# Loading wqk over two DMA queues, the second held by a memset, in a gated linear-attention and SwiGLU kernel

## The chip, the cores and the metric

The kernel runs on one core of a Trainium2 chip. The metric is the device time of one launch in microseconds; a lower one is better. The profile is a trace of one execution, with times in microseconds from the start of its span.

The engines are named as in the profile: PE is TensorE's matmuls and PEld its weight loads, DVE is VectorE, ACT is ScalarE, POOL is GpSimd, SP is SyncE. A "q" behind the name (SPq, ACTq) is that engine's sequencer, which issues DMAs in program order.

## The reference

One input `x` of 2048 tokens by 512 features feeds two branches, which a gate mixes. All tensors are bf16.

```python
def _A_ref(x, wqkv, wo):                      # linear attention, 32 heads of 16
    qkv = (x @ wqkv).reshape(B, S, 3, H, Dh).transpose(2, 0, 3, 1, 4)
    phi = lambda t: where(t > 0, t + 1, exp(t)) + 1e-6
    pq, pk = phi(q), phi(k)
    kv, z = einsum("bhsd,bhse->bhde", pk, v), einsum("bhsd->bhd", pk)
    o = einsum("bhqd,bhde->bhqe", pq, kv) / (einsum("bhqd,bhd->bhq", pq, z)[..., None] + 1e-6)
    return o.transpose(0, 2, 1, 3).reshape(B, S, D) @ wo

def _B_ref(x, w1, w3, w2):                    # SwiGLU, F = 1376
    return (silu(x @ w1) * (x @ w3)) @ w2

g = sigmoid((x * gate_w).sum(-1, keepdims=True))
return g * _A_ref(x, wqkv, wo) + (1 - g) * _B_ref(x, w1, w3, w2)
```

## The kernel before

The program is traced with a schedule written by hand: each engine runs its instructions in the order of the source, and semaphores are added where one engine reads or overwrites what another (or a DMA) has written. The contraction dimension of 512 is cut into KC = 4 pieces of 128, called kc below, and the tokens into NT = 16 tiles of 128.

**The start, up to about 9 us.** This is the stretch that the change touches. POOL makes small constants (`ident`, `ones`, the block mask `bmask` by a memset and two affine selects at L74 to L79, and the zeroed `hrem` tiles). SP issues the first DMAs in this order: the first 256 tokens of `x` in their natural layout (`xN`, L116), then the weights for q and k in four pieces of 128 rows by 1024 columns (`load_wqk`, L113, 256 KB each), then for each token tile from 2 to 15 a transposing DMA (`load_xT`, L110) with the natural rows of `x` in between (L128), then `wr`, `w1`, `w3`, `wv`, `wo` and `w2`. On ACT's own queue stands one small DMA, `touch` (L120), which reads 32 bytes from each row of wqkv's second and third piece; nothing reads the tile that it fills.

ACT loads its table and runs one tiny exponential (`act_pre`, L117) ahead of that DMA in program order. PE starts with 13 matmuls on constants (`warm_step`, L315). When `xN` is there, PE transposes the first two token tiles by matmuls with the identity (L321); DVE and ACT copy them from PSUM to `xT` (L335 to L338, and L350 for the last piece). Then come the projections of tiles 0 and 1 (L167), ordered by the weight piece that they need: for kc 0 the four of k and q, the transposes of kc 3, for kc 1 the four of k and q, then k alone for kc 2 (two matmuls), and k alone for kc 3. So each piece of `wqk` has a first reader: the 1st, the 5th, the 9th and the 11th projection matmul.

**After the start.** The projections, phi and the accumulation of the attention's G matrix (`g_step`) run token tile by token tile up to about 46 us. Then four token blocks of 512 run the SwiGLU (`glu_step`, which reads `w1` at L262 and `w3` at L268) and the outputs (`out_step`), with the attention's small products in between.

**DMA bookkeeping.** A DMA raises one of eight semaphores (102 to 109 in the trace), used in turn. From the ninth DMA on, an issue first waits for the landing of the DMA eight places before it.

Of the kernel before, what the change touches and what calls it, by code (L numbers as in the profile page):

```python
# [12 lines left out]
BF16 = mybir.dt.bfloat16  # L13
# [3 lines left out]
def kernel(  # L17
# [17 lines left out]
    nc = tc.nc  # L35
    P = nc.NUM_PARTITIONS

    Bb, S, D = A_x.shape
# [3 lines left out]
    KC = D // P  # L42
# [14 lines left out]
    wqkv_r = A_wqkv.rearrange("(kc d) n -> d kc n", d=P)  # L57
    w1_r = B_w1.rearrange("(kc d) f -> d kc f", d=P)
    w3_r = B_w3.rearrange("(kc d) f -> d kc f", d=P)

    consts = ctx.enter_context(tc.tile_pool(name="consts", bufs=1))
# [8 lines left out]

    ones = consts.tile([P, P], BF16, name="ones")
    nc.gpsimd.memset(ones[:], 1.0)
    bmask = consts.tile([P, HPC, Dh], BF16, name="bmask")
    nc.gpsimd.memset(bmask[:], 1.0)  # L74
    nc.gpsimd.affine_select(
        out=bmask[:], in_=bmask[:], pattern=[[-Dh, HPC], [0, Dh]], compare_op=ALU.is_ge,
        fill=0.0, base=0, channel_multiplier=1,
    )
    nc.gpsimd.affine_select(  # L79
        out=bmask[:], in_=bmask[:], pattern=[[Dh, HPC], [0, Dh]], compare_op=ALU.is_ge,  # L80
        fill=0.0, base=Dh - 1, channel_multiplier=-1,
# [10 lines left out]


    xN = consts.tile([P, NT, D], BF16, name="xN")
    wqk = consts.tile([P, KC, 2 * D], BF16, name="wqk")
    wq = wqk[:, :, 0:D]
    wk = wqk[:, :, D : 2 * D]
    wv = consts.tile([P, KC, D], BF16, name="wv")
# [2 lines left out]
    w1 = consts.tile([P, KC, F0], BF16, name="w1")  # L101
    w3 = consts.tile([P, KC, F0], BF16, name="w3")
# [3 lines left out]
    dq = nc.sync  # L106
# [3 lines left out]
        dq.dma_start(out=xT[:, :, ts], in_=x2d[ts, :], transpose=True)  # L110

    def load_wqk(kc):
        dq.dma_start(out=wqk[:, kc, :], in_=wqkv_r[:, kc, 0 : 2 * D])  # L113

    x_first = x2d[0 : 2 * P, :].rearrange("(p j) d -> p j d", j=2)
    dq.dma_start(out=xN[:, 0:2, :], in_=x_first)  # L116
    nc.scalar.activation(out=act_pre[:], in_=warm[:, 0:1], func=ACT.Exp)  # L117

    touch = consts.tile([P, 2, 16], BF16, name="touch")
    nc.scalar.dma_start(out=touch[:], in_=wqkv_r[:, 1:3, 0:16])  # L120
    for kc in range(KC):
        load_wqk(kc)
    natural = {3: (2, 4), 5: (4, 8), 7: (8, 12), 11: (12, 16)}
# [5 lines left out]
    with nc.allow_non_contiguous_dma(reason="gate column"):  # L129
        dq.dma_start(  # L130
            out=wr[:, :, 2 * FR : NR], in_=gate_w.rearrange("(kc d o) -> d kc o", d=P, o=1)
        )
    dq.dma_start(out=wr[:, :, 0:FR], in_=w1_r[:, :, F0:F])
    dq.dma_start(out=wr[:, :, FR : 2 * FR], in_=w3_r[:, :, F0:F])
    for w, w_r, cuts in ((w1, w1_r, (0, KC)), (w3, w3_r, (0, 2, KC))):
        for a, b in zip(cuts, cuts[1:]):
            dq.dma_start(out=w[:, a:b, :], in_=w_r[:, a:b, 0:F0])
    dq.dma_start(out=wv[:], in_=wqkv_r[:, :, 2 * D : 3 * D])
    dq.dma_start(out=wo[:], in_=A_wo.rearrange("(kc d) n -> d kc n", d=P))
# [358 lines left out]
```

## Time and profile before

| | |
|---|---|
| time, median of 3 runs | 179.68 us (179.66 to 179.94) |
| the profiled execution's own time | 179.22 us |
| its span, first to last instruction | 177.5 us |
| PE busy | 173.9 us (98%) |
| DVE, ACT, POOL busy | 100.5, 62.3, 62.9 us |
| mean DMA rate | 85 GB/s |
| granted TensorE clock | 1.0 in all slices |

The profiled execution's time is 1.72 us more than its span (launch and end) and 0.46 us less than the median. The page gives the busy share of each engine, the share of the DMA engines and the chain of work that ended last; a timeline gives the instructions of a stretch in order, each with the idle time of its engine before it and what ended that idle time in brackets. An issue's "us to landing" runs from its start on the issuing engine until its semaphore is complete.

### The profile page before, as it was taken

What the parts mean: (1) busy time and instruction counts of PE and PEld (TensorE: products, weight loads), DVE (VectorE), ACT (ScalarE), POOL (GpSimd) and SP (SyncE); (2) the same over time, 40 slices, a digit from 0 to 9 for tenths busy, and PEclk for the clock granted to TensorE, in tenths of its full rate; (3) what the DMA queues carried; (4) which work ended last, traced back from release to release, by engine and by line L of the source; (5) the groups of instructions that cost most, each with busy time, mean ns of one, the idle gap of its engine ahead of it and who ended that gap; (6) DMA issues with size and microseconds to landing.
All of it is one profiled execution on the core that took longest, in us unless ns stands there. A gap on an engine that the chain in (4) does not pass through costs nothing.

```text
span 177.5 us, 2504 instructions
## 1 busy us (share of the span) xinstructions
PE 173.9 (98%) x880; PEld 84.1 (47%) x880; DVE 100.5 (57%) x195; ACT 62.3 (35%) x113; POOL 62.9 (35%) x105
## 2 busy tenths in 40 slices
PE   8999999999999999999999999999999999999993
PEld 5444444444454464644444464444445444444453
DVE  1399788888899663575434166634325664433222
ACT  3354544444735441332342223142322223342130
POOL 5086656656577240446200044540004432000000
PEclk9999999999999999999999999999999999999999
DMA  5989869994002120233100013520000342000001
GB/s 174 269 202 216 163 106 264 406 381 142 4 0 59 30 47 16 59 82 96 30 0 4 0 40 80 90 63 0 0 0 30 89 92 59 0 0 0 30 33 59
DMA packets 28940, 15.15 MB, mean 85 GB/s; under 512 B 20896, under 2 KB 27264, under 8 KB 28928
## 3 DMA queue, kind: packets, MB, share of 16 engines
q1 hardware_dynamic: 28656, 14.98, 32.3%
q8 instruction: 7, 0.11, 0.3%
q14 instruction: 5, 0.04, 0.1%
q10 hardware_dynamic: 272, 0.01, 0.1%
HBM read 8.43 MB, written 2.10 MB: 59 GB/s over the span
## 4 chain that ended last, share of the span: by engine, by line
PE 98%; DVE 0%; issue 0%
PE bank L427 21%; PE bank L262 19%; PE bank L268 19%; PE bank L167 16%; PE bank L414 8%; PE bank L215 8%; PE bank L229 3%; PE bank L315 2%; PE bank L389 1%; PE bank L402 0%; PE bank L321 0%; DVE o L431 0%; PE bank L376 0%
## 5 line engine op out<-in xcount | busy, mean ns | idle before, releaser
L274 DVE TENSOR_TENSOR hT<-bank,sg 128x512 bf16<-128x512 f32 x40 | 27.2, 681 | 30.9 <-PE bank L268 30.9
L268 PE MATMUL bank<-xT,w 128*128 128x512 bf16 x160 | 41.1, 379 | 0.0
L262 PE MATMUL bank<-xT,w 128*128 128x512 bf16 x160 | 41.1, 379 | 0.0
L427 PE MATMUL bank<-w,hT 128*128 128x512 bf16 (+3 forms) x198 | 40.7, 355 | 0.0
L273 ACT ACTIVATE sg<-bank 128x512 bf16<-128x512 f32 x40 | 23.9, 597 | 46.9 <-PE bank L262 46.9
L296 POOL TENSOR_TENSOR pqs<-pq,rden 128x512 bf16<-128x512 bf16 x16 | 16.9, 1055 | 65.1 <-issue 60.0
L167 PE MATMUL bank<-wqk,xT 128*128 128x512 bf16 x128 | 30.6, 382 | 0.0
L431 DVE SCALAR_TENSOR_TENSOR o<-bank,omg_all,aga 128x512 bf16<-128x512 f32 (+2 forms) x18 | 12.5, 692 | 28.1 <-PE bank L427 28.0
L427 PEld LDWEIGHTS <-hT 128*128 128x128 bf16 (+1 forms) x198 | 18.5, 98 | 19.8
L199 POOL TENSOR_TENSOR zacc<-zacc,pk 128x128 f32<-128x128 f32 x56 | 23.3, 446 | 10.4 <-DVE pk L185 10.4
L268 PEld LDWEIGHTS <-w 128*128 128x128 bf16 x160 | 15.7, 98 | 18.9
L262 PEld LDWEIGHTS <-w 128*128 128x128 bf16 x160 | 15.6, 98 | 18.5
L419 ACT ACTIVATE aga<-bank,g_all 128x512 f32<-128x512 f32 x16 | 11.0, 687 | 28.9 <-PE bank L414 28.9
L167 PEld LDWEIGHTS <-xT 128*128 128x128 bf16 x128 | 12.5, 98 | 15.0 <-issue 0.5
L281 POOL TENSOR_TENSOR pr<-pq,zb 128x512 f32<-128x512 bf16 x16 | 18.4, 1153 | 1.7 <-DVE zb L377 1.7
L414 PE MATMUL bank<-M,pqT 128*128 128x512 bf16 x64 | 16.4, 378 | 0.0
L215 PE MATMUL bank<-pk,xN 128*128 128x512 bf16 x64 | 16.4, 379 | 0.0
L180 ACT ACTIVATE eq<-bank 128x512 bf16<-128x512 f32 x16 | 9.4, 597 | 16.0 <-PE bank L167 16.0
L185 DVE SCALAR_TENSOR_TENSOR pk<-bank,emk 128x512 bf16<-128x512 f32 x16 | 11.1, 692 | 1.6
L180 ACT ACTIVATE ek<-bank 128x512 bf16<-128x512 f32 x16 | 9.4, 597 | 6.6 <-PE bank L167 6.6
L185 DVE SCALAR_TENSOR_TENSOR pq<-bank,emq 128x512 bf16<-128x512 f32 x16 | 11.1, 692 | 0.6
L285 DVE TENSOR_REDUCE den<-pr 128x32 f32<-128x512 f32 x16 | 10.8, 676 | 0.0
(50 smaller groups left out, 81.7 us busy)
## 6 DMA issues: line engine op xcount, KB each, us to landing
w<-in_B_w_dram SPq DMA_DIRECT2D x4, 640.0 KB, 9.6
out_dram<-o SPq DMA_DIRECT2D x15, 128.0 KB, 1.9
xN<-in_A_x_dram SPq DMA_DIRECT2D x3, 512.0 KB, 4.5
w<-in_B_w_dram SPq DMA_DIRECT2D x1, 1280.0 KB, 7.6
wqk<-in_A_wqkv_dram SPq DMA_DIRECT2D x4, 256.0 KB, 3.7
xN<-in_A_x_dram SPq DMA_DIRECT2D x2, 256.0 KB, 2.9
wv<-in_A_wqkv_dram SPq DMA_DIRECT2D x1, 512.0 KB, 10.7
wo<-in_A_wo_dram SPq DMA_DIRECT2D x1, 512.0 KB, 11.1
```

The lines of the kernel that those rows point to most:

```text
L167: nc.tensor.matmul(ps[:], lhsT=xT[:, kc, t * P : (t + 1) * P], rhs=w[:, kc, :], start=(kc == 0), stop=(kc == KC - 1),)
L180: nc.scalar.activation(out=e[:], in_=ps[:], func=ACT.Exp)
L185: nc.vector.scalar_tensor_tensor(out=dst, in0=ps[:], scalar=0.0, in1=em[:], op0=ALU.max, op1=ALU.add)
L199: nc.gpsimd.tensor_tensor(out=(zaccb if t == NT - 1 else zacc)[:, cs], in0=zacc[:, cs], in1=pk[t][:, cs], op=ALU.add,)
L215: nc.tensor.matmul(bank[kc][:], lhsT=xN[:, t, kc * P : (kc + 1) * P], rhs=pk[t][:], start=(t == 0), stop=(t == NT - 1),)
L262: nc.tensor.matmul(g_ps[:], lhsT=w1[:, kc, fs], rhs=xT[:, kc, tok], start=(kc == 0), stop=(kc == KC - 1),)
L268: nc.tensor.matmul(u_ps[:], lhsT=w3[:, kc, fs], rhs=xT[:, kc, tok], start=(kc == 0), stop=(kc == KC - 1),)
L273: nc.scalar.activation(out=sg[:], in_=g_ps[:], func=ACT.Silu)
L274: nc.vector.tensor_tensor(out=hT[tb][:, fc, :], in0=u_ps[:], in1=sg[:], op=ALU.mult)
L281: nc.gpsimd.tensor_tensor(out=pr[t][:], in0=pq[:, t, :], in1=zb[:], op=ALU.mult)
L414: nc.tensor.matmul(a_ps[:], lhsT=pqT[:, c, ts], rhs=M2[:, c, :], start=(c == 0), stop=(c == KC - 1),)
L427: nc.tensor.matmul(b_ps[:, 0:w], lhsT=hT[tb][:n, fc, tl], rhs=w2[:n, fc, cs], start=(fc == 0), stop=(fc == FC),)
```

## The change

`wqk`'s pieces 1 and 3 are issued from ACT's queue, pieces 0 and 2 stay on SP's. A memset of one column of piece 1 is put on POOL, behind `bmask`'s first affine select. It writes where piece 1's DMA writes, so this DMA waits for it, and piece 3, which is next on ACT's queue, stands behind that wait. The DMA `touch` is left out. `w1` is loaded in two DMAs, kc 0 and 1 and then kc 2 and 3, as `w3` already is, in place of one; the number of DMAs stays the same.

```diff
     ones = consts.tile([P, P], BF16, name="ones")
     nc.gpsimd.memset(ones[:], 1.0)
+    wqk = consts.tile([P, KC, 2 * D], BF16, name="wqk")
     bmask = consts.tile([P, HPC, Dh], BF16, name="bmask")
     nc.gpsimd.memset(bmask[:], 1.0)
     nc.gpsimd.affine_select(
         out=bmask[:], in_=bmask[:], pattern=[[-Dh, HPC], [0, Dh]], compare_op=ALU.is_ge,
         fill=0.0, base=0, channel_multiplier=1,
     )
+
+    nc.gpsimd.memset(wqk[:, 1, 0:1], 0.0)
     nc.gpsimd.affine_select(
...
-    wqk = consts.tile([P, KC, 2 * D], BF16, name="wqk")
...
     def load_wqk(kc):
-        dq.dma_start(out=wqk[:, kc, :], in_=wqkv_r[:, kc, 0 : 2 * D])
+        q = nc.scalar if kc % 2 else dq
+        q.dma_start(out=wqk[:, kc, :], in_=wqkv_r[:, kc, 0 : 2 * D])
 
     x_first = x2d[0 : 2 * P, :].rearrange("(p j) d -> p j d", j=2)
     dq.dma_start(out=xN[:, 0:2, :], in_=x_first)
     nc.scalar.activation(out=act_pre[:], in_=warm[:, 0:1], func=ACT.Exp)
-
-    touch = consts.tile([P, 2, 16], BF16, name="touch")
-    nc.scalar.dma_start(out=touch[:], in_=wqkv_r[:, 1:3, 0:16])
     for kc in range(KC):
         load_wqk(kc)
...
-    for w, w_r, cuts in ((w1, w1_r, (0, KC)), (w3, w3_r, (0, 2, KC))):
-        for a, b in zip(cuts, cuts[1:]):
+    for w, w_r in ((w1, w1_r), (w3, w3_r)):
+        for a, b in ((0, 2), (2, KC)):
             dq.dma_start(out=w[:, a:b, :], in_=w_r[:, a:b, 0:F0])
```

## The prediction

> **What bounds the kernel now.** I read the page first, for the engine that sets the time.
>
> ```profile
> span 177.5 us, 2504 instructions
> PE 173.9 (98%) x880; PEld 84.1 (47%) x880; DVE 100.5 (57%) x195; ACT 62.3 (35%) x113; POOL 62.9 (35%) x105
> q10 hardware_dynamic: 272, 0.01, 0.1%
> ```
>
> PE is busy 98% of the span, and it also makes up 98% of the chain that ended last. A change of DMA queues leaves PE's work as it is, so it can only take or add PE's idle time. q10 is ACT's queue; it carries `touch` alone. Next I read the chain in order of time, for its first microseconds.
>
> ```profile
> 0.83 2.93 PE bank L315 x13
> 3.76 0.64 PE bank L321 x6
> 4.41 1.30 PE bank L167 x4
> 5.71 0.11 PE bank L321 x2
> 5.82 1.29 PE bank L167 x6
> ```
>
> The chain is PE's alone: 13 warm-up matmuls, 6 transposes, 4 projections of kc 0, 2 transposes, the projections of kc 1 and on. From 5.82 on there is one projection every 0.215 us (1.29 / 6). What PE waited for inside this is in the timeline of the same stretch.
>
> ```profile
> 0.80 0.40 SPq L116 DMA_DIRECT2D xN<-in_A_x_dram  x1
> 0.85 0.43 ACTq L120 DMA_DIRECT2D touch<-in_A_wqkv_dram  x1
> 1.25 1.83 SPq L113 DMA_DIRECT2D wqk<-in_A_wqkv_dram  x4
> 1.72 0.34 POOL L75 TENSOR_SCALAR_AFFINE_SELECT bmask<-bmask 128x128 bf16<-128x128 bf16 x1
> 3.13 2.58 SPq L110 DMA_TRANSPOSE xT<-in_A_x_dram  x2
> 3.56 0.84 PE L321 MATMUL bank<-ident,xN 128*128 128x128 bf16 x6
> 3.91 0.29 DVE L335 CAST xT<-bank 128x128 bf16<-128x128 f32 x1 [3.91 <-PE bank L321]
> 4.01 0.28 ACT L336 ACTIVATE xT<-bank 128x128 bf16<-128x128 f32 x1 [1.72 <-PE bank L321]
> 4.25 0.26 PEld L167 LDWEIGHTS <-xT 128*128 128x128 bf16 x2
> 4.40 1.30 PE L167 MATMUL bank<-wqk,xT 128*128 128x512 bf16 x4
> ```
>
> The first projection's weights are loaded at 4.25, right behind DVE's copy (3.91 + 0.29 = 4.20), but its matmul starts at 4.40. What came in between is the landing of `wqk`'s first piece, from the DMA issues of the four pieces, one query each:
>
> ```profile
> wqk<-in_A_wqkv_dram SPq DMA_DIRECT2D x1, 256.0 KB, 3.1
> wqk<-in_A_wqkv_dram SPq DMA_DIRECT2D x1, 256.0 KB, 3.5
> wqk<-in_A_wqkv_dram SPq DMA_DIRECT2D x1, 256.0 KB, 3.8
> wqk<-in_A_wqkv_dram SPq DMA_DIRECT2D x1, 256.0 KB, 4.0
> ```
>
> With the issues at 1.25, 1.72, 2.18 and 2.66, the landings are 4.36, 5.23, 6.03 and 6.69 (the trace's records; the lines round them). The first readers stand at 4.40, 5.65, 6.52 (four matmuls of 0.216 later) and 6.95 (two more). So piece 0 is late by 4.40 - 4.25 = 0.15 us, and the others have 0.42, 0.49 and 0.26 us in hand. `x` lands at 3.51, and PE is busy with the warm-ups until the transposes at 3.56. From 5.1 to 174.7 PE's starts show no other gap than one of 0.03 us. All that the change can win is that 0.15.
>
> **The change part by part.**
>
> `touch` goes. Its 272 packets took 0.1% of 16 engines' span, 0.09 to 0.27 us with the rounding; the records say 9 ns each, 272 x 9 / 16 = 0.15 us for each engine, between `x` and piece 0. I take 0.15: piece 0 lands at 4.21 in place of 4.36. `x` lands earlier too, hidden by the 13 warm-ups; without them it would show. What is late next is the copy, and the first projection starts at 4.25. The full 0.15 isn't kept: the first two projections stand 0.38 and 0.33 apart (starts 4.40, 4.78, 5.11) and all later ones 0.216. PE is still slow there, for (0.38 + 0.33 - 0.43) x 2 = 0.55 us, to about 4.95. If the speed-up comes at a fixed time, the 0.15 won are slow time, worth half. The gain is 0.08 to 0.15; I take 0.10. It can be 0 too, should piece 0 not follow `touch` (below), and no more than 0.15.
>
> The memset is 128x1; four of that shape on POOL took 0.1 us each at the start. It runs behind L75's end (1.72 + 0.34 = 2.06), so to about 2.16. It delays L79 and `hrem`'s memsets by up to 0.1, and POOL's next instruction with a reader in haste is `zacc` at 9.08, after 5.68 us idle: nothing. If that cover were gone, 0.1.
>
> Pieces 1 and 3 on ACT's queue. Piece 1 is issued at about 2.2 in place of 1.72, 0.5 later; piece 3 behind it, 2.2 + 0.43 + 0.04 = 2.7, as before (2.66). Queued behind the waiting issue on ACT is the copy L336 at 4.01: ACT's sequencer is free at 3.1, so 0.9 us hide it. `act_pre` stands ahead and doesn't hold the queue: `touch` was issued at 0.85 during the table load. Piece 2 moves up to 1.72 on SP. Where the pieces land isn't shown by any row, so bounds: piece 1 lands at 5.08 if only its place in the line counts (5.23 - 0.15) and at 5.58 if the 0.5 count in full; its reader comes at 5.55 (5.65 - 0.10). Cost 0 to 0.03; I take 0. Piece 2 lands between 5.08 and 6.03 for a reader at 6.42: 0. Piece 3 lands at 6.69 - 0.15 + 0.04 = 6.58 for a reader at 6.85: 0.27 in hand.
>
> What SP issues behind the pieces moves up by the two issues that left, 0.95 us: the transposes start at 2.18 in place of 3.13. They sit on SP's queue and pieces 1 and 3 on the other, so they no longer stand behind piece 3. The landings of pieces 3, xT 2 and xT 3 were 6.69, 7.29 and 7.71, thus one transpose ahead of piece 3 costs it 0.60 and two cost 1.02. Against 0.27 in hand that is PE idle for 0.33 or 0.75; none ahead costs 0. I take 0: xT 2's issue takes 1.28, to 3.46, and piece 3's ends at 3.1. The transposes' first reader is tile 2 at 8.24; earlier is of no use. The trace of the DMA engines over that time gives one queue at work, hence no row for two.
>
> `w1` in two pieces: one more issue of 0.5 us on SP at 26 us, in exchange for the issue of `touch` in the count of eight semaphores, which shifts by one between them. `w1` landed at 33.9, its reader L262 comes at 46.5, 12.6 us later: 0 in either direction. Were that cover gone, 0.5.
>
> Sum: -0.10. Against the profiled execution's 179.22 (span 177.50, and 1.72 around it) that is 179.12; against the median, 0.46 above it, 179.58. About 0.2% (0.36 us) can be told from no change.
>
> [...] A DMA that ACT issues beside one of SP's has one row: `touch` took 0.43 while SP issued `xN` in 0.40, and SP's issues alone took 0.41 to 0.43, so neither waited; a transpose's issue of 1.28 beside one of ACT's has no row. [...]
>
> **The rivals.**
>
> First, slower: ACT's issues wait for SP's transposes. xT 2's issue (2.18 to 3.46) starts within 0.1 us of piece 1's. If it goes first, piece 1 is issued at 3.46 and lands 2.7 (as `x`, with nothing ahead) to 3.1 later, 6.2 to 6.6, with a reader at 5.55: 0.6 to 1.0 idle. If xT 3 (to 5.2) also precedes piece 3, that one lands at 7.9 for a reader at 6.85 + 0.6: 0.45 more, and L336 on ACT stands behind its issue. Price 0.6 to 1.4, about 1.0, less 0.10: 180.6. It decides once piece 1 is issued after 2.9. For: the two issues collide almost exactly. Against: `touch` and `xN` did not wait for each other.
>
> Second, about the same or slower: issues run, but transposes get ahead of piece 3 on the DMA engines. One ahead gives 179.68 - 0.10 + 0.33 = 179.9, two 180.3. For: the transposes now start 0.95 earlier on a queue of their own. Against: piece 3 is issued before them in full.
>
> Third, no change: piece 0 lands at 4.36 still, because its start is set by its own issue at 1.25 or because piece 1 shares its engines: 179.68.
>
> Fourth, faster by more: the median is 0.46 above the profiled execution. If that is a wait at the start for `wqk` that this trace doesn't show, an earlier line of pieces could win it: 179.2. Nothing in the trace shows it.
>
> **How the numbers follow.** The forecast has 0.34, the first rival 0.25, the second 0.20 (half of it within 0.2%), no change 0.07, the fourth 0.14. Faster is the fourth, 0.14; slower is the first and half of the second, 0.35; within 0.2% is 0.34 + 0.07 + 0.10 = 0.51. The range goes from the fourth case's 179.2 to the first rival's 180.6, leaving out the longer half of that rival and some of the fourth. The likeliest case's own range is 179.5 to 179.7.
>
> **What would show it.** Right: the first projection at 4.25, no gap at the readers of pieces 1 and 3, no q10 before 2.2, ACT's two issues of 0.43 each done by 3.2, PE busy unchanged. First rival: an issue of L113 on ACTq of a microsecond or more, or starting after 3. Second: piece 3 landing after 6.9 and a gap at the 11th projection. The prediction is wrong if the first projection starts later than 4.40, or PE's spacing of 0.216 begins later than 5.11.

## The result and the profile after

The changed kernel takes 187.16 us (median of 6 runs, 185.68 to 187.92) against 179.57 us (6 runs, 179.22 to 179.94) for the kernel before: a ratio of 1.041 [1.0384, 1.0437], 7.6 us slower. The prediction said 179.6 us in a range of 179.2 to 180.6.

In the page of the changed kernel, the span, the busy times, PE and its granted clock in 40 slices, and ACT's DMA queue:

```profile
span 185.8 us, 2490 instructions
PE 176.0 (95%) x864; PEld 84.6 (46%) x880; DVE 99.9 (54%) x195; ACT 62.1 (33%) x113; POOL 63.0 (34%) x106
PE   8169999999999999999999999999999999999994
PEclk9957999999999999999999999999999999999999
q10 hardware_dynamic: 288, 0.52, 1.5%
```

The whole loss lies in slices 2 to 4 (4.6 to 18.6 us). PE is almost idle in the second slice, and its granted clock drops in the third and fourth. From there on every slice of PE is full, as before. The chain of work that ended last, over the same start (start, length, what):

```profile
2.20 1.28 SPq L112
...
3.52 3.47 DMA xT<-in_A_x_dram
...
7.08 4.91 DMA wqk<-in_A_wqkv_dram
...
12.03 5.59 PE bank L167 x16
```

Before the change this chain was PE's alone. Now it runs from SP's transposing DMA of token tile 3 (issued at 3.52, landed at 7.00) to ACT's DMA of `wqk`'s piece 1, which starts only at 7.08 and lands at 11.99, and then to PE. No data passes between those two DMAs: what links them is a semaphore. The timeline of the stretch shows what that does to ACT and PE:

```profile
2.01 0.10 POOL L81 MEMSET wqk<- 128x1 bf16 x1
...
4.34 1.03 PE L167 MATMUL bank<-wqk,xT 128*128 128x512 bf16 x2
...
7.08 1.85 ACTq L116 DMA_DIRECT2D wqk<-in_A_wqkv_dram  x2
...
8.97 0.28 ACT L336 ACTIVATE xT<-bank 128x128 bf16<-128x128 f32 x1 [6.67 <-DMA xN<-in_A_x_dram]
...
9.30 1.03 PE L167 MATMUL bank<-wqk,xT 128*128 128x512 bf16 x2 [3.93 <-ACT xT L336]
...
12.03 5.16 PE L167 MATMUL bank<-wqk,xT 128*128 128x512 bf16 x14 [1.48 <-DMA wqk<-in_A_wqkv_dram]
```

The memset that holds piece 1 ends at 2.11, so by the data piece 1 could go at 2.2. It goes at 7.08. The second issue on ACT's queue (piece 3) starts at 8.58. The bracket behind ACT's copy L336 names what ended ACT's idle time: not PE, whose transposes are long done, but the landing of the natural `x` rows, `xN(2:4)`, at 8.56. For that landing ACT's queue waited, and the copy stood behind it. PE has two projections at 4.34, then nothing for 3.93 us until that copy, then waits another 1.48 us for piece 1.

The semaphores in the trace explain it. Eight DMAs of SP take 102 to 109: `xN`, piece 0, piece 2, xT 2, xT 3 (106), `xN(2:4)` (107), xT 4 and xT 5. The next four of SP, up to `xN(8:12)`, take 102 to 105 again. Pieces 1 and 3 take 106 and 107: the held DMAs come 13th and 14th in the turn, though they stand third and fifth in the source. The turn isn't the time of issue either, as xT 6 and xT 7, places 10 and 11, are issued at 8.61 and 9.85. What rule makes it isn't in the trace. It seems to be fixed with the program: in experiment 4 piece 1 is issued ahead of xT 5 and yet has 106 of the second round, where xT 5 has 109 of the first. In it a held DMA stands late. By the rule that an issue waits for the landing of the DMA eight places before, piece 1 waits for xT 3 (landed 6.995, issue at 7.08) and piece 3 for `xN(2:4)` (landed 8.562, issue at 8.58).

The loss adds up in the profiled execution (187.65 us). The fifth projection, the first reader of piece 1, starts at 12.03 instead of 5.65: 6.38 later. Then PE runs at half its clock, with projections 0.427 us apart instead of 0.216, up to 16.17: ten spacings take 4.13 us where full speed needs 2.16, which is 1.97. Together 8.35, and PE's last instruction ends at 183.07 instead of 174.72, 8.35 later.

### The profile page after: what moved, and what is told of

Read it like the earlier page. It is cut to its first block, busy times and chain, and to the rows that moved or that the text cites. A ratio compares the mean times of both kernels' runs of the same rounds, so it can differ in the third digit from the quotient of the medians.

```text
span 185.8 us, 2490 instructions
## 1 busy us (share of the span) xinstructions
PE 176.0 (95%) x864; PEld 84.6 (46%) x880; DVE 99.9 (54%) x195; ACT 62.1 (33%) x113; POOL 63.0 (34%) x106
## 4 chain that ended last, share of the span: by engine, by line
PE 92%; DMA 5%; SPq 1%; issue 1%; DVE 0%; ACTq 0%
PE bank L427 20%; PE bank L262 19%; PE bank L268 18%; PE bank L167 15%; PE bank L215 7%; PE bank L414 7%; PE bank L229 3%; DMA wqk<-in_A_wqkv_dram 3%; DMA xT<-in_A_x_dram 2%; SPq L112 1%; PE bank L389 0%; PE bank L402 0%; SPq L116 0%; SPq L119 0%; DVE o L431 0%
## 5 line engine op out<-in xcount | busy, mean ns | idle before, releaser
L262 PE MATMUL bank<-xT,w 128*128 128x512 bf16 x158 | 41.0, 379 | 0.3
L427 PE MATMUL bank<-w,hT 128*128 128x512 bf16 (+4 forms) x197 | 40.6, 355 | 0.1
L268 PE MATMUL bank<-xT,w 128*128 128x512 bf16 x154 | 40.3, 379 | 0.2
L167 PE MATMUL bank<-wqk,xT 128*128 128x512 bf16 x126 | 33.2, 405 | 5.5 <-ACT xT L336 3.9
L427 PEld LDWEIGHTS <-hT 128*128 128x128 bf16 (+1 forms) x198 | 18.6, 98 | 19.8
```

Of the source, the lines that this page charges most:

```text
L167: nc.tensor.matmul(ps[:], lhsT=xT[:, kc, t * P : (t + 1) * P], rhs=w[:, kc, :], start=(kc == 0), stop=(kc == KC - 1),)
L262: nc.tensor.matmul(g_ps[:], lhsT=w1[:, kc, fs], rhs=xT[:, kc, tok], start=(kc == 0), stop=(kc == KC - 1),)
L268: nc.tensor.matmul(u_ps[:], lhsT=w3[:, kc, fs], rhs=xT[:, kc, tok], start=(kc == 0), stop=(kc == KC - 1),)
L427: nc.tensor.matmul(b_ps[:, 0:w], lhsT=hT[tb][:n, fc, tl], rhs=w2[:n, fc, cs], start=(fc == 0), stop=(fc == FC),)
```

## The experiments

Twelve kernels, each as an edit of the kernel after (1 to 5 and 9 to 11) or before (6 to 8 and 12). Tile declarations that move or are added are left out of the edits shown, and line numbers shift by a few lines from kernel to kernel. A ratio is to the kernel before, run again beside each group of experiments (medians 179.63 to 179.81 us). In the expectations, A is the theory of the semaphores' turn. B says that a second queue is slow by itself, through a wait at issue while SP issues transposes, or because the transposes pass the pieces on the DMA engines. C says that plain pieces on ACT's queue and SP's transposes in flight together slow each other far beyond sharing.

### 1. The transposes held by a memset too

```diff
     nc.gpsimd.memset(wqk[:, 1, 0:1], 0.0)
+    nc.gpsimd.memset(xT[:, 0, 2 * P : 2 * P + 1], 0.0)
```

The transposes now also wait for POOL, so pieces 1 and 3 take earlier semaphores (106 and 109, both in the first round; the eight are 102 to 104 and 106 to 110 here) and wait for no landing.

> The changed kernel with one line more: a second one-column memset, on xT at token 256, so that SP's first transposing DMA waits for POOL as long as ACT's first piece does. The hold, ACT's queue and all else stay; only the turn of the eight semaphores changes, since ACT's two pieces now come ahead of the transposes in it and wait for no landing. Theory A (ACT's two issues wait for the landings of xT 3 and of xN's tiles 2 and 3, whose semaphores they take over, and everything else follows from that): ACT issues at 2.2 and 2.7, pieces 1 and 3 land by 5.6 and 7.0, PE has no gap over 0.4 us, 179.4 to 180.0. Theory B (a second queue is slow by itself: the issue on ACT waits while SP issues transposes, or the transposes pass the pieces on the DMA engines): ACT's issues after 3.5 or pieces landing after 7.5, 181 or more, the larger part of the 7.6 us lost stays.

Measured: 183.14 us, 180.43 to 185.15. Three runs (180.43, 181.75, 181.92) kept PE's clock at 1.0; in the other three (184.4 to 185.2), the profiled one among them, it was halved for a time. The ratio of the first three is 1.0095 [1.0059, 1.0132]; no trace shows when their pieces landed. The timeline of the profiled run:

```profile
2.15 0.86 ACTq L117 DMA_DIRECT2D wqk<-in_A_wqkv_dram  x2
2.20 2.59 SPq L113 DMA_TRANSPOSE xT<-in_A_x_dram  x2
...
7.97 2.29 PE L168 MATMUL bank<-wqk,xT 128*128 128x512 bf16 x5 [2.46 <-DMA wqk<-in_A_wqkv_dram]
```

Both issues run at 2.15 and 2.56 and take 0.38 and 0.46 us, while SP's transposing issue of 1.29 us starts at 2.20. So A holds, with the issue at the time that the prediction wanted, and no wait for SP's issue shows. But the pieces still come late: piece 1 lands at 7.93, 5.8 us after its issue, piece 3 at 9.87, 7.3 after, where pieces took 3.1 to 4.0 before the change. PE waits 2.46 us. A explains 12.03 - 7.97 = 4.06 us at the fifth projection; 7.97 - 5.65 = 2.32 us remain for B or C. Landings scatter on one queue too, so not all of it need be the second queue's: with all pieces on SP's queue and no `touch` the fifth projection starts at 5.63 with the hold (experiment 11) and at 6.36 without it (experiment 8).

### 2. No hold

```diff
-    nc.gpsimd.memset(wqk[:, 1, 0:1], 0.0)
```

> The changed kernel without the memset on wqk. ACT issues pieces 1 and 3 at about 0.85 and 1.3, with semaphores of their own. Theory A: no wait for a landing, so most of the loss goes; pieces 1 and 3 run beside x and piece 0, which may land up to 0.7 later (one piece's time): 179.5 to 180.5. Theory B: ACT's queue still costs, 181 or more.

Measured: 180.34 us (180.02 to 182.52), ratio 1.0078 [1.0045, 1.0111]. The runs fall into two groups, 180.0 to 180.4 and 181.7 to 182.5; the profile is of the first, and what makes the second is open. ACT issues at 0.86 and 1.27, and in the trace the last packet of pieces 1 and 3 starts at 5.39, ahead of the first transposing packet at 5.58. The waits of PE in the first 12 us:

```profile
PE bank L320 <- DMA xN<-in_A_x_dram: 0.5, 1, 0.5
PE bank L166 <- DMA wqk<-in_A_wqkv_dram: 0.3, 1, 0.3
```

Here two queues move 399 GB/s from 3.6 to 4.8 us, so a second queue is not slow by itself. What it costs is that `x` lands at 4.21 instead of 3.51: it now has the DMA engines together with piece 1, whose first packet starts at 2.67.

### 3. ACT's two copies on DVE

```diff
-    nc.scalar.activation(out=xT[:, 0, P : 2 * P], in_=bank[1][:, 0:P], func=ACT.Copy)
+    nc.vector.tensor_copy(out=xT[:, 0, P : 2 * P], in_=bank[1][:, 0:P])
...
-    nc.scalar.activation(out=xT[:, 2, 0 : 2 * P], in_=bank[3][:, 0 : 2 * P], func=ACT.Copy)
+    nc.vector.tensor_copy(out=xT[:, 2, 0 : 2 * P], in_=bank[3][:, 0 : 2 * P])
```

> The changed kernel with the two copies behind the waiting issues on ACT (L336 and L338) moved to DVE. PE then no longer waits for ACT at 4.8 to 9.3. If that wait is what the change costs, some 4 us come back: 183. If what counts is the landing of pieces 1 and 3 at 12.0 and 14.2, PE waits for piece 1 right away and the time stays at 186.5 to 187.8.

Measured: 186.85 us, ratio 1.0393 [1.0356, 1.043]. The waits of PE in the first 17 us:

```profile
PE bank L167 <- DMA wqk<-in_A_wqkv_dram: 4.8, 1, 4.8
```

The 3.93 us for the copy are gone and come back as a wait for piece 1 itself, which landed at 11.02. The blocked copy is the larger of the two waits in the profile after, yet it costs almost nothing: it ends first, and the landing ends last.

### 4. PE kept busy while it waits

```diff
+            if kc == 0 and (n, t) == ("k", 1):
+                fill(36)
+            if kc == 1 and (n, t) == ("k", 0):
+                fill(14)
```

`fill(n)` runs n matmuls of the warm-up's kind.

> The changed kernel with 36 matmuls on constants ahead of the third projection and 14 ahead of the fifth, in PE's idle time, so that its clock isn't halved. By the trace of the changed kernel the 11th projection could start at piece 3's landing, 14.2, in place of 14.55, and run at 0.216 a projection at once: 1.1 us less than the changed kernel, about 186.1. If the halved clock (9.2 to 16.1) is the main cost, up to half of that stretch comes back, 3.4 us, 183.8.

Measured: 184.95 us (184.66 to 185.37), ratio 1.0297 [1.0273, 1.032]. The granted clock stays at 1.0, and 2.2 us come back, which fits the 1.97 counted above. In the profiled executions the fifth projection starts at 11.83 instead of 12.03 and PE ends 2.19 earlier, which is the 0.20 and 1.98 for the clock. Piece 1 landed at 9.79 in this profile, but that won nothing, since the 14 matmuls held the fifth projection until 11.83. With the clock undisturbed in both, experiment 1 against this one gives A as 184.95 - 181.75 = 3.2 us. Up to 0.6 of that is the fill's own: piece 3 landed at 12.47, and its reader started at 13.12.

### 5. The transposes held until piece 3 has landed

```diff
         load_wqk(kc)
+    nc.gpsimd.tensor_copy(out=xT[:, 0, 2 * P : 2 * P + 1], in_=wqk[:, 3, 0:1])
```

> The changed kernel with a one-column POOL copy from wqk's piece 3 to the place of xT that SP's first transposing DMA writes, so that no transpose is issued before piece 3 has landed; as in the run with SP held, ACT's pieces then come early in the semaphores' turn. Theory A alone (waits for landings) says nothing new of the pieces here. Theory C (plain pieces on ACT's queue and transposes on SP's, in flight together, slow each other down far beyond sharing): pieces 1 and 3 land by 5.6 and 6.8 with no slow stretch, no gap over 0.3 us at their readers, and the transposes, issued at about 6.8, land at 9.3 and 10.5, 1.0 to 1.3 us late for tiles 2 and 3: 180.4 to 181.2. If pieces 1 and 3 still land after 7.5, the second queue is slow without the transposes and C is wrong.

Measured: 181.26 us, ratio 1.0088 [1.0059, 1.0117]. Pieces 2, 1 and 3 land at 6.29, 6.48 and 7.03. The waits of PE in the first 12 us:

```profile
PE bank L168 <- DMA xT<-in_A_x_dram: 0.9, 1, 0.9
PE bank L168 <- DMA wqk<-in_A_wqkv_dram: 0.3, 1, 0.3
```

Without transposes in flight, piece 1 lands 4.3 us after its issue instead of 5.8 and piece 3 4.5 instead of 7.3. The transposes then come too late for tile 2 and cost 0.9. Even so the pieces are no earlier than on one queue (5.23, 6.03 and 6.69 in the kernel before), and they lie between what C and its opposite forecast, so this run alone doesn't decide C.

### 6 and 7. A spare 256 KB DMA beside the transposes, on ACT's queue or on SP's

```diff
+    nc.scalar.dma_start(out=spare[:], in_=wqkv_r[:, 0, 0 : 2 * D])
```

In 6 it stands on ACT behind L338. In 7 the same DMA is issued by SP between xT 4 and xT 5. Nothing reads it.

> The kernel before with one plain DMA more, 256 KB of wqkv into a tile that nothing reads, issued from ACT behind the copy L338 (its semaphore makes it wait for piece 3, so it is issued at about 6.7, while SP issues the transposes of tiles 4 and 5). Theory C: it takes over 4.5 us to land, and xT 4 and xT 5 land at least 1.5 us later than the 10.04 and 10.67 of the kernel before; with tile 4's reader at about 11.9, 179.6 to 182. If the queues only share the engines, xT 4 and 5 land 0.7 later, 10.8 and 11.4, and the time stays within 0.3 of the kernel before.

> The same spare DMA, but issued from SP between the transposes of tiles 4 and 5, hence on one queue with them. All theories: it adds its own transfer, 0.7 us, and its issue, 0.4 us: it lands within 3.5 us, xT 5 at 11.2 to 11.8, and the time stays within 0.3 of the kernel before.

Measured: 179.98 us (1.0024 [1.0003, 1.0046]) on ACT, 179.8 us (0.9997 [0.9977, 1.0017]) on SP. The spare DMA took 4.2 us from issue to landing on ACT and 3.1 on SP, and xT 5 landed at 12.58 and 11.40, against 10.67 without it. The second queue is the slower one, but the difference lies between what C and sharing gave, and decides nothing. The profile of 6 also has a surprise: before the spare DMA is issued, piece 1 lands at 6.85 instead of 5.23, on SP's one queue. From 6.0 to 7.5 its DMA engines moved 115 GB/s, against 183 in the kernel before. So a stretch this slow, with pieces and transposes in flight, occurs on one queue too. And 6 bears A out in a kernel without a hold: ACT is done with the copy in front at 4.98, but the spare DMA, which takes over piece 3's semaphore 107, is issued at 8.22, right behind that piece's landing at 8.20.

### 8. The kernel before without `touch`, and with `w1` in two pieces

```diff
-    touch = consts.tile([P, 2, 16], BF16, name="touch")
-    nc.scalar.dma_start(out=touch[:], in_=wqkv_r[:, 1:3, 0:16])
...
-    for w, w_r, cuts in ((w1, w1_r, (0, KC)), (w3, w3_r, (0, 2, KC))):
+    for w, w_r, cuts in ((w1, w1_r, (0, 2, KC)), (w3, w3_r, (0, 2, KC))):
```

> The two other parts of the change alone: the kernel before without touch and with w1 in two pieces; all four pieces of wqk stay on SP's queue without a hold. The prediction's own terms: piece 0 lands at 4.21 in place of 4.36, first projection at 4.25, 0.10 less, 179.4 to 179.6 beside 179.57. If it is slower by over 0.36, these parts share in the loss.

Measured: 179.9 us, ratio 1.0012 [0.9994, 1.0029]: no gain, and no loss that can be told from none. The first projection stands at 4.37. Piece 1 lands at 6.32 in this profile, 1.1 later than in the kernel before though issued at the same time on the same queue, and PE waits for it:

```profile
6.36 3.69 PE L165 MATMUL bank<-wqk,xT 128*128 128x512 bf16 x16 [0.84 <-DMA wqk<-in_A_wqkv_dram]
```

The stretch from 3.6 to 4.8 us of this kernel (its length, PE's busy time and matmuls, PE's clock, the DMA engines' share, which can pass 1, and GB/s):

```profile
3.60:4.80 1.20, 1.20 (x9) 1.00 0.78 205
```

and the same of the kernel before:

```profile
3.60:4.80 1.20, 1.20 (x9) 1.00 0.98 338
```

The DMA engines move less here without `touch`. They move 338, 314, 343 and 278 GB/s in the four profiles with it (before, 6, 7, 12), and 169 to 293 in nine of the ten without; the tenth, experiment 2, which has all four pieces issued by 2.2 us, moves 399. Of the ten only 8 and 11 have all four pieces on SP's queue, as the four with `touch` do; they have 205 and 203. Whether `touch` is the cause isn't shown: no experiment tests it by itself.

### 9. Tiles 2 to 5 of `x` loaded plainly

Experiment 1, with plain loads for the tiles that SP has in flight beside the pieces. The transposition of these four tiles is left out.

```diff
         ts = slice(t * P, (t + 1) * P)
+        if t < 6:
+            dq.dma_start(out=xT[:, :, ts], in_=x2d[ts, :].rearrange("p (kc q) -> p kc q", q=P))
+            return
```

> The run with SP held, but the loads of xT's tiles 2 to 5 are plain DMAs of the same bytes in place of transposing ones (the kernel leaves out the transposition of these four tiles, so what it computes from them is not the reference's). Pieces 1 and 3 still go over ACT's queue beside SP's loads. Theory C (transposes in flight beside plain pieces of the other queue slow everything): the pieces land by 6.5 and 7.5, the DMA rate between 4.8 and 7.5 us stays above 250 GB/s (237 and 109 with SP held), 179.6 to 181. If two queues are slow whatever they carry, the rate stays under 200 and the time at 181.5 or more.

Measured: 181.0 us, ratio 1.0059 [1.0039, 1.0079]. The stretch from 6.0 to 7.5 us, in the same columns, for experiment 1:

```profile
6.00:7.50 1.50, 0.00 (x0) 0.86 0.61 109
```

and for this kernel:

```profile
6.00:7.50 1.50, 0.10 (x1) 1.00 1.09 333
```

With transposes beside the pieces the rate falls to 109 GB/s; with plain loads on the same two queues it is 333. (SP's plain loads take 0.55 to 0.88 us to issue, so the later ones start earlier than the transposes did.) C is right on the rate in these two profiles. Piece 1 lands at 7.36 instead of 7.93, piece 3 at 8.27 instead of 9.87.

What this is worth in time isn't settled. All six runs here kept the clock, where three of six did in experiment 1. Against the median of those three the gain is 0.7 us (181.75 to 181.0), but they spread from 180.43 to 181.92, and the two intervals overlap. PE still waits 1.4 us for piece 1 here; why isn't shown.

### 10. The hold later

The memset of piece 1 behind `hrem`'s memsets.

> The changed kernel with the memset behind hrem's two memsets, so it ends at about 3.5 in place of 2.1. Theory A: the hold itself isn't felt, since ACT's first issue waits for xT 3's landing at 7.0 anyhow; but piece 3 now gets a later turn of the semaphores and waits for xT 5's landing (12.2 in the changed kernel) in place of xN's (8.6): it lands at 15 to 16.5 in place of 14.2, and the time is 188.5 to 190.5. Without theory A, 1.4 us more hold at most, and nothing where the pieces are late for another reason: 186.5 to 188.6.

Measured: 188.96 us (188.5 to 190.08), ratio 1.0516 [1.0482, 1.055]. Piece 3 now takes 109, behind xT 5. The chain of work that ended last:

```profile
6.70 3.86 DMA xT<-in_A_x_dram
...
10.57 5.54 DMA wqk<-in_A_wqkv_dram
...
16.16 3.99 PE bank L167 x10
```

The memset ends 1.35 us later than in the kernel after, at 3.46. That moves piece 3's issue from 8.58 to 10.57, behind the landing of xT 5 (10.55). Piece 1 keeps 106, and its issue, at 6.84, again follows xT 3's landing (6.76). Piece 3 lands at 16.12; A had forecast 15 to 16.5, and 188.5 to 190.5 us. In both kernels, and in experiments 3 and 4 too, each of ACT's two issues starts 0.02 to 0.08 us after the landing that A names.

### 11. All four pieces on SP, with the hold

```diff
-        q = nc.scalar if kc % 2 else dq
-        q.dma_start(out=wqk[:, kc, :], in_=wqkv_r[:, kc, 0 : 2 * D])
+        dq.dma_start(out=wqk[:, kc, :], in_=wqkv_r[:, kc, 0 : 2 * D])
```

> The changed kernel with all four pieces issued by SP: the hold, the missing touch and w1's two pieces stay, the second queue goes. SP waits for the memset at 2.15 and issues pieces 1 to 3 from 2.2 to 3.5, then the transposes, 0.45 later than the kernel before; no issue up there waits for a landing. If the loss comes from the second queue (by the waits for landings and by what it carries beside the transposes), this is 179.5 to 180.3. If holding piece 1 costs by itself, 181 or more.

Measured: 180.3 us (180.01 to 180.6), ratio 1.0033 [1.0019, 1.0047]. The memset, the missing `touch` and the split of `w1` are all in it, and only the second queue is undone: that alone wins back 187.16 - 180.3 = 6.9 of the 7.6 us. Experiment 2, which undid only the hold, won back 6.8, so the loss needs both together. PE waits 0.31 and 0.62 us for pieces 1 and 2, which land at 5.59 and 7.24.

### 12. The natural rows of `x` ahead of the transposes

```diff
+    dq.dma_start(out=xN[:, 2:4, :], in_=x_t[:, 2:4, :])
-    natural = {3: (2, 4), 5: (4, 8), 7: (8, 12), 11: (12, 16)}
+    natural = {5: (4, 8), 7: (8, 12), 11: (12, 16)}
```

This puts plain rows between the pieces and the first transpose, in the kernel before.

> The kernel before with xN's tiles 2 and 3 loaded ahead of the transposes of tiles 2 and 3, so that 256 KB of plain rows stand between piece 3 and the first transpose. If the pieces' landings in the kernel before are now and then held up by the first transposes (piece 1 landed at 6.3 and 6.9 in two of the runs with all pieces on SP, 5.2 in two others), this is 0.2 to 0.5 less than the kernel before, 179.2 to 179.5, with xT 2 landing at 7.6 to 8.0 for a reader at 8.24. Otherwise 179.6 to 179.9.

Measured: 179.7 us, ratio 0.9995 [0.998, 1.001]. Pieces 1 to 3 land at 5.19, 6.45 and 7.10, xT 2 at 8.35. Nothing is won, since in the kernel before PE has no wait there to lose. No kernel here is faster than the one before by more than the noise.

## Why the prediction was wrong

**The step that failed.** "Piece 1 is issued at about 2.2 in place of 1.72, 0.5 later; piece 3 behind it" took the hold to end with the memset. The memset did end when it should, at 2.11 (predicted 2.16). But the issue also waited for its semaphore, 106, to come free with xT 3's landing (6.995), and the two held DMAs took later places in the turn, the 13th and 14th. Piece 1 was issued at 7.08, 4.9 us after the forecast, piece 3 at 8.58, 5.9 after. The prediction spoke of "the count of eight semaphores" only for `w1`. That pieces 1 and 3 wait for no landing holds only if the turn is that of the source, and the trace before already spoke against that: `touch` stands ahead of piece 0 in the source, yet has semaphore 104 where piece 0 has 103. Experiment 1 moves the places and the issues are at 2.15 and 2.56; experiment 10 moves them the other way and the issue follows the next landing.

**What followed from it.** "The copy L336 ... 0.9 us hide it" fell with the same step, as ACT was held to 8.92 instead of 3.1. Experiment 3 shows that this costs next to nothing while the landing is late anyway (187.16 against 186.85). The halved clock was not foreseen at all; it adds 1.97 in the profiled execution.

**"The transposes ... I take 0".** This term was too small even with the issues on time. The prediction's bounds for piece 1 were 5.08 to 5.58. Experiment 11, with the issue at 2.15 on SP's queue, has 5.59; on ACT's queue it is 7.93 (experiment 1). One queue doesn't secure those bounds either: piece 1 landed at 6.32 in experiment 8 and at 6.85 in experiment 6. The second rival named the transposes among the pieces, but priced them at 0.33 to 0.75 by adding landings from a one-queue trace, and put them on piece 3 alone. Against the kernel before, pieces on two queues cost 1.1 to 2.4 us beside transposes (the interval of experiment 1's three runs with the clock undisturbed) and 0.7 to 1.4 beside plain loads (experiment 9). With all pieces on one queue it is 0.3 to 0.8 (experiment 11).

**The first rival** had the right place, ACT's issue, and the right point of decision, an issue after 2.9. Its cause was wrong, and so was its price of 0.6 to 1.4. It had ACT's issues wait for SP's transposing issues; in experiment 1 ACT's two, at 2.15 and 2.56, take 0.38 and 0.46 us beside SP's of 1.29 (2.20 to 3.49), so neither waited for it.

**`touch`, -0.10.** Experiment 8 has no gain, 1.0012 [0.9994, 1.0029]; piece 0 landed at 4.32 there instead of the forecast 4.21, and the first projection stood at 4.34 in the kernel after and 4.37 in experiment 8, against the forecast of 4.25 and the 4.40 of before. Piece 0 did land earlier in the kernel after, at 4.235, but then the copies set the start. "What is late next is the copy" was right; that the copy stands still at 4.20 was not, since `x` landed 0.11 later than before (3.62).

**Right:** the memset's 0.1 us, nothing for `w1` (its two parts landed at 30.66 and 32.45, long ahead of the reader at 54.82), an issue time of 0.4 for each piece, and that there was almost nothing to win.

**How the 7.6 us divide,** by medians, when one part is undone after the other: the halved clock 2.2 (experiment 4), the semaphores' turn 3.2 (experiment 4 to 1, with the fill's share in it), the transposes beside the pieces 0.7 (experiment 1 to 9), the second queue beside plain loads 0.7 (experiment 9 to 11), the hold 0.4 (experiment 11 to 8), and 0.3 left for `touch` and `w1`. The first two are clear of the noise. The steps of 0.7 and less aren't, since the intervals of neighbours overlap; only the second queue with transposes beside it, as a whole, is (experiment 1 to 11). The shares also depend on the order: undoing the hold alone wins 6.8, undoing the second queue alone 6.9, and in the profiles of both (experiments 2 and 11) the clock isn't halved, so the 2.2 of the halved clock is in each.

**Open:** why the DMA engines move only 109 GB/s (experiment 1) and 115 GB/s (experiment 6, on one queue) from 6.0 to 7.5 us, with pieces and transposes in flight, and whether `touch` changes the rate behind it.

## What to carry to other kernels

Before a DMA is held back or moved to another queue, work out which semaphore it will take over, from the semaphore numbers in a trace and not from the source: a held DMA can inherit a wait for a transfer that it has nothing to do with (here 4.9 us for piece 1), and what stands behind it on that engine waits too (here the copy L336, with ACT idle for 6.67 us). A DMA that may wait doesn't belong on the queue of an engine with copies to do that PE needs soon. In this kernel the pieces that are needed first did best alone in one queue ahead of the transposing DMAs; a second queue saves issue time (0.4 us each here), but with it `x` landed 0.7 us later in experiment 2, and piece 1 5.8 us after its issue in experiment 1.

## What the runs showed of the hardware that was not expected

**A clock that halved while PE was partly busy.** PE's clock in experiment 1, in two windows around its drop:

```profile
3.68:7.09 3.41, 1.58 (x13) 1.00 1.03 195
7.09:13.92 6.83, 5.95 (x15) 0.50 1.17 247
```

In the records of the granted clock, changes lie 3.41 us or a multiple of it apart (5.83, 9.24 and 16.07 in the kernel after). There PE was idle for all of the 3.41 us before the drop at 9.24. In experiment 1 PE was busy for 1.58 of the 3.41 us before the drop, 46%; the first 1.6 us of its wait of 2.46 us lie in that window. Then it ran at half clock for 6.83 us. In the first half of these PE was busy for 2.53 of 3.41 us, and the clock stayed at half; in the second it was busy throughout, and the clock rose at its end. In the 3.41 us of experiment 9 that hold its wait of 1.44 us PE was busy for 58%, and the clock stayed at 1.0:

```profile
5.42:8.83 3.41, 1.97 (x11) 1.00 1.13 309
```

Why only three of experiment 1's six runs were halved isn't shown: none of the other three has a trace.

**The clock's rise wanders.** PE comes to full speed at 3.57 to 6.32 us in the fourteen profiles, at 5.00 in that of before. The PEclk row reads 1.0 ahead of it too; it is the projections that tell, 0.38 to 0.43 us apart until then and 0.216 after. An edit of 0.1 us at the start is lost in that.

**The first packet on ACT's queue often comes late.** From issue to first packet, the first DMA on ACT's queue took 1.03 us (experiment 10) to 2.02 us (`touch` in experiment 6) in the twelve traces that have one, 1.92 in the kernel before and 1.56 in the kernel after. SP's load of `x`, with no DMA of the kernel ahead of it, took 1.01 to 1.38. Whether that is the queue or the traffic already on the DMA engines isn't shown.
